# Four-block q and k loads of one head pair, moved from SyncE's queue to ScalarE's, one block a slot

## The chip, the cores and the metric

The kernel runs on one core of a Trainium2 chip. The metric is the device time of one launch in microseconds (us). The time shown for a kernel is the median of several runs; one further execution was taken with the hardware profiler, and all rows of the profile are of that one execution. PE is TensorE, DVE VectorE, ACT ScalarE, POOL GpSimd and SP SyncE. A name with a q behind it (SPq, ACTq) is the engine's instruction queue while it issues a DMA.

## The reference: hashed attention, then a gated feed-forward layer

```
# q, k, v: 4 batches, 8 heads, 768 tokens, 64 dims; proj: 64 x 6 (float32)
bits    = (q @ proj > 0), (k @ proj > 0)             # 6 bits each: a bucket of 0 to 63
mask    = q_bucket[:, None] == k_bucket[None, :]
scores  = where(mask, q @ k.T / 8, -1e9)
attn    = exp(scores - rowmax); attn /= attn.sum(-1) + 1e-9
x       = (attn @ v), heads side by side             # 3072 tokens x 512
xn      = x / sqrt(mean(x*x) + 1e-6) * rms_g
g       = xn @ w_gate                                # 512 x 1536
out     = (g * sigmoid(g) * (xn @ w_val)) @ w_out    # 3072 x 512
```

## The kernel before

**Slots.** The work is cut into 192 slots. A slot is two score matmuls (L343: 128 keys by 384 queries each) of one head and one half of a batch, called a wave w (w = 2 x batch + half). ScalarE turns them into exponentials (`probs`, L353), and TensorE multiplies these by v (L365) some slots later. Slots 0 to 47 hold batch 0, slots 48 to 71 wave 2 and slots 72 to 95 wave 3, which are the two halves of batch 1. Within a wave there are three slots a head. Slot s of the written order begins with the scores of number s+1, so `probs(54)` is issued in slot 53.

**The layer behind it.** From slot 48 on, every 24 slots carry the feed-forward layer of a finished wave: 12 gate steps (matmuls into g_ps L445, a tanh on ScalarE L447), 12 value steps (v_ps L455, two VectorE operations L457 and L458), then the output projection (y_ps L469).

**Making q and k ready.** A head pair (b, hp) of q or k is loaded as float32. For batch 0 and the first two pairs of batch 1 TensorE transposes it. From pair (1, 2) on it is loaded in four blocks of 32 partitions (`load_blocks`, L121; 768 pieces of 128 bytes each), and VectorE transposes it (`turn_dve`, L193, four operations for k and four for q); each operation reads all four blocks. GpSimd casts the result into the tile QK (L201). `hash_lone` (b = 1, hp = 2 and 3) then makes the sign bits with TensorE (d_ps L209) and VectorE (L216), and SyncE copies them into 12 rows of QK by eight small DMAs (L284). The pairs (1, 0) and (1, 1) do the same through `hash_pair`, with eight DMAs each (L267). These DMAs are called A1 to A8 for pair (1, 0) and B1 to B8 for pair (1, 1) below; A1 and A2 are needed by `scores(48)`, B1 and B2 by `scores(54)`, B3 by `scores(55)`, B4 and B5 by `scores(57)`.

**What sets the order.** The order on each engine is written out: `at(s, f, ..., rank=r)` puts a step into slot s, lower ranks first, and `probs` comes behind ranks under 3. Every engine runs its instructions in that order. The table `work` gives for each pair the slots of its k, q and v loads, of the transposes, the casts and the hash. The load tiles come from one pool of ten buffers, in turn.

**Which semaphore a DMA waits for.** As the program is built, the DMAs of SyncE and of ScalarE share eight completion semaphores, dealt out in turn over both queues together, and a DMA is not issued until the earlier DMA that holds its semaphore has landed. Before the change nearly all these DMAs are SyncE's own. A7 waits for the v load of pair (1, 1) and A8 for that of pair (1, 2). The four k blocks of pair (1, 3) follow B8 on SyncE, then come its q blocks, its v load, the k blocks of pair (2, 0) and the eight hash DMAs of pair (1, 2).

Of the kernel before, what the change touches and what calls it, by code (L numbers as in the profile page):

```python
# [43 lines left out]
def kernel(  # L44
# [12 lines left out]
    nc = tc.nc  # L57
# [38 lines left out]
    raw = {}  # L96

    def raw_tile(b, hp, which):
        shape = [128, 24, 32] if which != "v" and (b, hp) not in BY_PE else [128, 2, 6, D]
        raw[b, hp, which] = lpool.tile(shape, FP32, name=which + "L", tag="L")  # L100
        return raw[b, hp, which]
# [10 lines left out]
        else:  # L112
            eng.dma_start(out=t[:, heads[0]], in_=src[:, heads[0]])

    def load_blocks(eng, b, hp, which):
        lt = raw_tile(b, hp, which)
        for hh in range(2):
            src = {"q": q, "k": k}[which][b, 2 * hp + hh].rearrange("(t k) d -> t k d", k=24)
            for dc in range(2):
                p0 = 64 * hh + 32 * dc  # L120
                eng.dma_start(out=lt[p0 : p0 + 32], in_=src[:, :, 32 * dc : 32 * dc + 32])  # L121

# [448 lines left out]
    def at(s, f, *a, rank=3):  # L573
        plan[s].append((rank, len(plan[s]), lambda: f(*a)))
# [56 lines left out]
    def in_row(loads, s, hash_slot=None):  # L631
        return loads, range(s, s + 8), (s + 4, s + 8, s + 9), hash_slot

    work = {
        (1, 2): ((21, 23, 30), (36, 37, 40, 40, 48, 49, 50, 51), (42, 52, 46), 53),
        (1, 3): in_row((42, 44, 47), 52, 61),
        (2, 0): in_row((51, 56, 59), 61), (2, 1): in_row((64, 67, 70), 71, 80),
        (2, 2): in_row((73, 76, 79), 81), (2, 3): in_row((82, 85, 88), 91, 100),
        (3, 0): in_row((94, 98, 102), 106), (3, 1): in_row((104, 108, 112), 116, 125),
# [1 line left out]
    }  # L641
    for (b, hp), (loads, turns, cast_slots, sh) in work.items():
        for which, s in zip("kqv", loads):
            at(s, load_rows if which == "v" else load_blocks, nc.sync, b, hp, which)
        for i, s in enumerate(turns):
            at(s, turn_dve, b, hp, "kq"[i // 4], i % 4, rank=5)
        for which, s in zip("kq", cast_slots):
            at(s, cast_pool, b, hp, which)
        if sh:
            if b == 1:  # L650
                at(sh, hash_lone, b, hp)
            else:
                at(sh, hash_pairs, b, (hp - 1, hp))
        at(cast_slots[2], v_prep, b, hp)
        at(cast_slots[2], v_sum, b, hp)
        if hp % 2:
            at(66 if b == 1 else 48 * b + (17 if hp == 3 else -4), v_mean, b, hp - 1, 4)
# [100 lines left out]
```

## Time and profile before

| | us |
|---|---|
| median of 3 runs (337.58 to 343.3) | 340.42 |
| the profiled execution, its own time | 339.3 |
| its span, first to last instruction | 337.5 |
| TensorE matmul busy in it | 326.8 |
| VectorE busy | 236.4 |
| ScalarE busy | 210.0 |
| GpSimd busy | 155.3 |

The profiled execution's own time is 1.8 us longer than its span, which is what lies around the instructions. The granted TensorE clock is 0.999 over the span. Four views are used below. The busy table by stretches of time shows how full each engine is. The waits tell who waited for whom. The chain of waits goes back from the last instruction to what released each step. The timeline lists instructions in order of time: start, duration, engine, line, operation, output and input, how many were merged into the row, and in square brackets the idle time before it with its releaser. Where a row merges several, the duration is from the first start to the last end. A DMA row on SPq or ACTq is the time that the queue needed to issue it, not the transfer.

### The profile page before, as it was taken

Reading aid. Unit: us, or ns where it says so; the run is one execution under the profiler, and the core shown is the slowest. Engines: PE = TensorE matmul, PEld = TensorE weight load, DVE = VectorE, ACT = ScalarE, POOL = GpSimd, SP = SyncE. Lnnn points to the kernel's source line nnn. Section 1 sums busy time; section 2 is a strip of 40 time slices with the busy share of each in tenths; the row PEclk is TensorE's granted clock in tenths of the full one; section 3 lists DMA queues with packets and bytes.
Section 4 is the critical chain, followed back from the end, with each engine's and each line's share of the span. In section 5 each row is a group of like instructions: output and inputs, shape, how many; then the busy total and the mean of one; then the engine's idle time right before and its main releaser. Section 6 shows DMA issues by size and latency. Waiting matters only on the chain.

```text
span 337.5 us, 7796 instructions
## 1 busy us (share of the span) xinstructions
PE 326.8 (97%) x2993; PEld 201.0 (60%) x2993; DVE 236.4 (70%) x526; ACT 210.0 (62%) x328; POOL 155.3 (46%) x230
## 2 busy tenths in 40 slices
PE   8999989889999999999999999999999999999995
PEld 7566656455566565566555666566556665655653
DVE  4769798688758896668768897557546663883860
ACT  3789987656666575757666676567667675332321
POOL 4878789836465576245736475613111311110000
PEclk9999999999999999999999999999999999999999
DMA  7999999464376064508243261100010001001002
GB/s 238 330 223 260 169 169 187 75 124 100 79 186 118 15 111 119 104 20 168 69 105 84 44 116 64 35 16 0 33 62 2 3 0 64 33 0 64 32 0 93
DMA packets 80244, 31.36 MB, mean 93 GB/s; under 512 B 65240, under 2 KB 77264, under 8 KB 80208
## 3 DMA queue, kind: packets, MB, share of 16 engines
q1 hardware_dynamic: 76272, 26.09, 31.7%
q0 software_dynamic: 3712, 4.72, 8.8%
q8 instruction: 23, 0.38, 0.5%
q14 instruction: 13, 0.11, 0.1%
q10 hardware_dynamic: 224, 0.07, 0.1%
HBM read 28.32 MB, written 6.29 MB: 103 GB/s over the span
## 4 chain that ended last, share of the span: by engine, by line
PE 85%; DVE 6%; SPq 3%; DMA 2%; ACT 2%; issue 1%; DVEq 0%; ACTq 0%
PE y_ps L469 18%; PE v_ps L455 17%; PE s_ps L343 15%; PE g_ps L445 12%; PE o_ps L365 9%; PE s_ps L445 5%; PE d_ps L209 4%; SPq L267 2%; PE t_ps L169 1%; PE x_ps L430 1%; PE z_ps L336 1%; DMA kL<-in_k_dram 1%; DVE otmp L380 1%; DVE xn L423 1%; ACT psb L353 1%
## 5 line engine op out<-in xcount | busy, mean ns | idle before, releaser
L353 ACT ACTIVATE psb<-s_ps 128x768 f16<-128x768 f32 x192 | 150.8, 808 | 28.1 <-PE s_ps L343 26.9
L343 PE MATMUL s_ps<-QK 76*128 76x384 f16 x384 | 93.5, 325 | 1.3 <-ACT psb L353 0.5
L455 PE MATMUL v_ps<-xnT,wv 128*128 128x384 f16 x384 | 78.1, 326 | 0.1
L469 PE MATMUL y_ps<-wo,ht 128*128 128x512 f16 x276 | 69.2, 379 | 0.3 <-ACT ysb L476 0.3
L389 POOL TENSOR_TENSOR x<-otmp,rcp 128x384 f32<-128x384 f32 x31 | 25.7, 830 | 93.0 <-DVE rcp L385 92.7
L365 PEld LDWEIGHTS <-psb 128*128 128x128 f16 x1152 | 51.6, 97 | 25.5 <-issue 7.5
L447 ACT ACTIVATE t<-g_ps 128x384 f32<-128x384 f32 x72 | 35.3, 490 | 43.6 <-PE g_ps L445 43.4
L458 DVE SCALAR_TENSOR_TENSOR ht<-a,v_ps 128x384 f16<-128x384 f32 x96 | 53.2, 554 | 10.7 <-PE v_ps L455 1.5
L457 DVE SCALAR_TENSOR_TENSOR a<-t,g_ps 128x384 f32<-128x384 f32 x72 | 39.5, 548 | 28.5 <-ACT t L447 28.3
L445 PE MATMUL g_ps<-xnT,wg 128*128 128x384 f16 x288 | 58.6, 325 | 0.7 <-DVE a L457 0.5
L365 PE MATMUL o_ps<-vl,psb 128*128 128x65 f16 x1152 | 56.8, 194 | 0.6 <-DVE otmp L380 0.5
L455 PEld LDWEIGHTS <-wv 128*128 128x128 f16 x384 | 36.4, 97 | 23.9 <-issue 0.5
L445 PEld LDWEIGHTS <-wg 128*128 128x128 f16 x384 | 36.0, 97 | 24.4 <-issue 1.1
L343 PEld LDWEIGHTS <-QK 76*128 76x128 f16 x384 | 31.6, 98 | 16.1 <-issue 3.7
L469 PEld LDWEIGHTS <-ht 128*128 128x128 f16 x276 | 25.9, 97 | 24.0 <-issue 0.6
L476 ACT COPY ysb<-y_ps 128x512 f32<-128x512 f32 x23 | 13.5, 585 | 25.5 <-PE y_ps L469 22.8
L431 DVE TENSOR_TENSOR xnT<-x_ps,gcol 128x512 f16<-128x512 f16 x24 | 16.3, 685 | 15.1 <-PE x_ps L430 15.1
L401 POOL TENSOR_TENSOR sq<-x 128x384 f32<-128x384 f32 x31 | 25.6, 826 | 2.4
L380 DVE TENSOR_TENSOR otmp<-o_ps,cvb 128x390 f32<-128x390 f32 x32 | 17.8, 558 | 8.8 <-PE o_ps L365 8.7
L447 ACT ACTIVATE t<-s_ps 128x384 f32<-128x384 f32 x24 | 11.8, 491 | 18.4 <-PE s_ps L445 17.6
L201 POOL CAST QK<-kT 64x768 f16<-64x768 f32 x20 | 16.8, 838 | 12.4 <-DVE kT L193 6.5
L193 DVE STREAM_TRANSPOSE kT<-kL 128x192 f32<-128x192 f32 x40 | 19.8, 517 | 2.7 <-DMA kL<-in_k_dram 2.7
(80 smaller groups left out, 325.7 us busy)
## 6 DMA issues: line engine op xcount, KB each, us to landing
vL<-in_v_dram SPq DMA_DIRECT2D x16, 384.0 KB
out_dram<-ysb SPq DMA_DIRECT2D x23, 256.0 KB
kL<-in_k_dram SPq DMA_DIRECT2D x40, 96.0 KB
qL<-in_q_dram SPq DMA_DIRECT2D x40, 96.0 KB
kL<-in_k_dram SPq DMA_DIRECT2D x5, 384.0 KB
qL<-in_q_dram SPq DMA_DIRECT2D x5, 384.0 KB
wg<-in_moe_w_gate_dram POOLq DMA_DIRECT2D x2, 768.0 KB, 7.2
wv<-in_moe_w_val_dram POOLq DMA_DIRECT2D x2, 768.0 KB, 8.5
```

The costliest lines, as they stand in the source:

```text
L343: nc.tensor.matmul(ps[:, j, 0:HALF], k_cols(w // 2, h, 2 * p + j), q_cols(w, h), start=True, stop=True,)
L353: nc.scalar.activation(psb[w, h][:, p], sps.pop(g)[:, :, 0:HALF], AF.Exp, scale=ESCALE,)
L365: nc.tensor.matmul(o[:, c, hh, 0:65], psb[w, h][:, jt // 2, jt % 2, 128 * c : 128 * c + 128], vls[b % 2][:, h, v_chunk(b, h, jt), 0:65], s ...
L380: nc.vector.tensor_add(tmp[:, :, :, 0:65], o[:, :, :, 0:65], cvb[b % 2][:, 2 * hp : 2 * hp + 2, 0:65].unsqueeze(1).to_broadcast([128, 3, 2 ...
L389: eng.tensor_mul(xd.rearrange("p c (h d) -> p c h d", h=2), tmp[:, :, :, 0:64], r.to_broadcast([128, 3, 2, 64]),)
L401: nc.gpsimd.tensor_mul(sq, xd, xd)
L445: nc.tensor.matmul(g, wg[:, kt, fs], xnT[w][:, kt], start=(kt == 0), stop=(kt == 3))
L447: nc.scalar.activation(t, g, AF.Tanh, scale=0.5)
L455: nc.tensor.matmul(vv, wv[:, kt, fs], xnT[w][:, kt], start=(kt == 0), stop=(kt == 3))
L457: nc.vector.scalar_tensor_tensor(out=a, in0=t, scalar=1.0, in1=g, op0=ALU.add, op1=ALU.mult)
L458: nc.vector.scalar_tensor_tensor(out=ht[w][:, ft], in0=a, scalar=0.5, in1=vv, op0=ALU.mult, op1=ALU.mult)
L469: nc.tensor.matmul(y, ht[w][:, ft, c * 128 : (c + 1) * 128], wo[:, ft, :], start=(ft == 0), stop=(ft == NF - 1),)
```

## The change

`load_blocks` can now load some of its four blocks (`parts`), and makes the tile at the first call. Only pair (1, 3) is loaded otherwise: its k blocks are issued by ScalarE's queue in slots 46, 47, 48 and 49 and its q blocks in slots 50 to 53, one block a slot and as the last step of the slot (rank 6). Before, SyncE issued the four k blocks in slot 42 and the four q blocks in slot 44. The v load of the pair stays on SyncE in slot 47; in the pool of load tiles it now comes between k and q.

```diff
-    def load_blocks(eng, b, hp, which):
-        lt = raw_tile(b, hp, which)
-        for hh in range(2):
+    def load_blocks(eng, b, hp, which, parts=range(4)):
+        lt = raw.get((b, hp, which)) or raw_tile(b, hp, which)
+        for i in parts:
+            hh, dc = divmod(i, 2)
             src = {"q": q, "k": k}[which][b, 2 * hp + hh].rearrange("(t k) d -> t k d", k=24)
-            for dc in range(2):
-                p0 = 64 * hh + 32 * dc
-                eng.dma_start(out=lt[p0 : p0 + 32], in_=src[:, :, 32 * dc : 32 * dc + 32])
+            eng.dma_start(out=lt[32 * i : 32 * i + 32], in_=src[:, :, 32 * dc : 32 * dc + 32])
...
-        (1, 3): in_row((42, 44, 47), 52, 61),
+        (1, 3): in_row((46, 50, 47), 52, 61),
...
-            at(s, load_rows if which == "v" else load_blocks, nc.sync, b, hp, which)
+            if which == "v":
+                at(s, load_rows, nc.sync, b, hp, which)
+            elif (b, hp) == (1, 3):
+                for i in range(4):
+                    at(s + i, load_blocks, nc.scalar, b, hp, which, [i], rank=6)
+            else:
+                at(s, load_blocks, nc.sync, b, hp, which)
```

The order of the compute instructions on TensorE, VectorE, ScalarE and GpSimd is the same in both built programs; the eight loads go from SyncE's list into ScalarE's. On ScalarE the order there becomes: `probs(47)`, k0, `probs(48)`, k1, tanh 0, `probs(49)`, k2, tanh 1, `probs(50)`, k3, `probs(51)`, tanh 2, q0, `probs(52)`, q1, tanh 3, `probs(53)`, q2, tanh 4, `probs(54)`, q3, `probs(55)`, tanh 5, `probs(56)`, where k0 to q3 are the blocks.

The eight semaphores are dealt out anew, now over both queues. As built, these DMAs wait for these to have landed:

| DMA (queue) | waits for the landing of |
|---|---|
| k0 (ACT) | a k block of pair (1, 2), issued 20 slots earlier |
| A7 (SP) | v load of pair (1, 2) |
| A8 (SP) | k0 |
| k1 (ACT) | A2 |
| k2 (ACT) | k1 |
| k3 (ACT) | B3 |
| q0 (ACT) | B4 |
| q1 (ACT) | B7 |
| q2 (ACT) | k2 |
| q3 (ACT) | q0 |
| fourth k block of pair (2, 0) (SP) | v load of pair (1, 3) |
| first hash DMA of pair (1, 2) (SP) | k3 |

## The prediction

> **What bounds the kernel now.** I read the busy totals first, then the waits, then the chain, then the timelines of single engines.
>
> ```profile
> PE 326.8 (97%) x2993; PEld 201.0 (60%) x2993; DVE 236.4 (70%) x526; ACT 210.0 (62%) x328; POOL 155.3 (46%) x230
> ```
>
> TensorE is busy for 326.8 of 337.5 us. A change that only moves loads can win no more than idle time of TensorE. The busy table by stretches shows where there is some near the change.
>
> ```profile
> 50.00:57.20 7.20, 6.52 (x80) 4.39 (x80) 5.87 (x10) 5.34 (x8) 6.70 (x10) 1.00 1.20 224
> 57.20:61.50 4.30, 4.30 (x43) 2.79 (x42) 3.85 (x10) 3.58 (x7) 4.14 (x6) 1.00 0.12 25
> 61.50:66.60 5.10, 5.10 (x49) 2.63 (x47) 2.84 (x7) 3.32 (x6) 4.81 (x8) 1.00 0.61 97
> 66.60:69.10 2.50, 0.34 (x2) 0.12 (x2) 1.77 (x4) 0.25 (x1) 0.34 (x1) 1.00 0.96 144
> 69.10:76.00 6.90, 6.90 (x65) 4.47 (x65) 6.02 (x14) 4.30 (x8) 2.80 (x4) 1.00 0.58 116
> ```
>
> The columns are the stretch, its length, busy PE, PEld, DVE, ACT and POOL, granted clock, DMA share, GB/s. TensorE is full from 57.2 to 66.6 and again from 69.1; in the 2.50 us between it works 0.34. So 2.16 us are the prize. The waits from 57 to 76 us name the cause:
>
> ```profile
> DVE kT L193 <- DMA kL<-in_k_dram: 2.7, 1, 2.7
> PE m_ps L324 <- DVE bits L216: 1.6, 1, 1.6
> PE g_ps L445 <- DVE a L457: 0.5, 1, 0.5
> ```
>
> VectorE waits 2.7 us for k of pair (1, 3), and TensorE behind it 1.6 + 0.5. The chain tells why k is late:
>
> ```profile
> 60.56 0.72 SPq L267
> ...
> 61.39 0.65 SPq L121
> ...
> 63.86 3.29 DMA kL<-in_k_dram
> ...
> 67.28 0.52 DVE kT L193
> 67.79 0.45 DVE bits L216
> ...
> 69.10 0.82 PE g_ps L445 x4
> ...
> 72.83 1.79 DMA QK<-bits
> ```
>
> SyncE issues hash DMAs up to B8 at 60.56 and only then the k blocks. A block lands 3.29 us after its issue begins, a hash DMA 1.79.
>
> **Part 1: what SyncE loses, and its new wait.** Its timeline and one of its waits:
>
> ```profile
> 54.42 6.86 SPq L267 DMA_DIRECT2D QK<-bits  x9
> ...
> 61.39 3.06 SPq L121 DMA_DIRECT2D kL<-in_k_dram  x4
> 64.56 2.64 SPq L121 DMA_DIRECT2D qL<-in_q_dram  x4
> ...
> 71.15 6.18 SPq L284 DMA_DIRECT2D QK<-bits  x8
> ```
> ```profile
> SPq L267 <- DMA vL<-in_v_dram: 2.3, 1, 2.3
> ```
>
> Eight issues leave SyncE, 61.39 to 67.20, so 5.8 us of its queue. But A8, the first of the nine at 54.42, will wait for k0. The nine take 6.86/9 = 0.76 us each, so B3 is issued 3 x 0.76 = 2.28 after A8 and lands 1.79 later: 4.1 us after k0 has landed.
>
> When k0 lands follows from ScalarE's timeline and the weight load beside it:
>
> ```profile
> 50.94 3.66 ACT L353 ACTIVATE psb<-s_ps 128x768 f16<-128x768 f32 x5 [0.38 <-PE s_ps L343]
> 55.13 0.81 ACT L353 ACTIVATE psb<-s_ps 128x768 f16<-128x768 f32 x1 [0.53 <-PE s_ps L343]
> ```
> ```profile
> 47.75 0.82 POOL L526 DMA_DIRECT2D wo<-in_moe_w_out_dram  x1
> ```
> ```profile
> wo<-in_moe_w_out_dram POOLq DMA_DIRECT2D x2, 768.0 KB, 10.3
> ```
>
> The five are `probs(43)` to `probs(47)`; k0 stands behind them, so its issue begins at 50.94 + 3.66 = 54.60. The nearest price of a landing is 3.29, which gives 57.9. But the DMA engines are full to 57.2 (share 1.20) with a weight load that lands at 47.75 + 10.3 = 58.05, while the 3.29 was taken at a share of 0.61 to 0.96. If none of k0's data moved before that load is done, the 1.50 by which a block (3.29) is longer than a hash DMA (1.79) comes on top: 59.5. I take 58.3, just behind the weight load, with 57.9 and 59.5 as bounds. Then B3 lands at 58.3 + 4.1 = 62.4. Between A8's old issue at 54.42 and its new one at 58.3 SyncE stands still for 3.9 us and gives back most of its 5.8. Two score rows of TensorE, `scores(53)` and `scores(54)`, tell whether that hurts at once:
>
> ```profile
> 61.47 0.49 PE L343 MATMUL s_ps<-QK 76*128 76x384 f16 x2
> ...
> 63.37 0.49 PE L343 MATMUL s_ps<-QK 76*128 76x384 f16 x2
> ```
>
> B1 and B2 land by 58.35 + 2 x 0.76 + 1.79 = 61.7, before `scores(54)` at 63.4, so TensorE does not feel it directly.
>
> **Part 2: what ScalarE gains to do.** An issue on ACTq occurs twice in the trace, for other shapes:
>
> ```profile
> 0.72 0.55 ACTq L483 DMA_DIRECT2D pn<-in_proj_dram  x1
> ```
> ```profile
> 334.47 0.35 ACTq L726 DMA_DIRECT2D out_dram<-ysb  x1
> ```
>
> SyncE paid 0.65 for this shape (the L121 row). Bounds are 0.35 and 0.65 in calm queues; I take 0.65, the same shape. Eight are 5.2 us. The cover is ScalarE's idle time, in brackets below, some tenths at a time and 3.10 in the old stall:
>
> ```profile
> 57.27 0.81 ACT L353 ACTIVATE psb<-s_ps 128x768 f16<-128x768 f32 x1
> 58.51 0.49 ACT L447 ACTIVATE t<-g_ps 128x384 f32<-128x384 f32 x1 [0.44 <-PE g_ps L445]
> 58.90 1.51 ACT L353 ACTIVATE psb<-s_ps 128x768 f16<-128x768 f32 x2
> 60.69 0.49 ACT L447 ACTIVATE t<-g_ps 128x384 f32<-128x384 f32 x1 [0.28 <-PE g_ps L445]
> ...
> 66.04 0.81 ACT L353 ACTIVATE psb<-s_ps 128x768 f16<-128x768 f32 x1 [0.30 <-PE s_ps L343]
> 69.95 0.49 ACT L447 ACTIVATE t<-g_ps 128x384 f32<-128x384 f32 x1 [3.10 <-PE g_ps L445]
> 70.33 0.81 ACT L353 ACTIVATE psb<-s_ps 128x768 f16<-128x768 f32 x1
> ```
>
> A tanh holds the next instruction back 0.39 (58.51 to 58.90), a probs 0.75 (1.51/2). Now step by step:
> - k0 from 54.60 to 55.25 moves `probs(48)` by 0.1, k1 runs 56.06 to 56.71 in a gap. No cost.
> - k2 needs k1: 56.06 + 3.29 = 59.35, issued to 60.00. Tanh 1 moves from 58.51 to 60.00 and `probs(50)` ends at 60.00 + 0.39 + 0.75 = 61.14. ScalarE is 1.5 late, but the next wait covers this one.
> - k3 needs B3: issued 62.4 to 63.05. `probs(51)` ends at 63.8 instead of 58.90 + 1.51 = 60.41. Queued behind k3 are tanh 2 and everything later on ScalarE; TensorE has two score banks, so `scores(53)` needs the bank that `probs(51)` frees. It moves from 61.5 to 63.8: TensorE stands 2.3 us, in the place of the old 2.16.
> - From 63.05 to the start of `probs(56)` ScalarE runs without a gap: five probs (51 to 55), four tanh (2 to 5), four issues (q0 to q3): 5 x 0.75 + 4 x 0.39 + 4 x 0.65 = 7.9, so 70.95. It was 70.33: 0.6 late. q0 and q1 add no wait: B4 and B7 land at 63.2 and 65.4, ScalarE arrives at 64.2 and 65.6; q2 and q3 wait for blocks issued more than 3.29 us before.
>
> TensorE agrees: its 5.1 us of work from 61.5 to 66.6, begun at 63.8, ends at 68.9, and the gate step of 69.10 follows some tenths later, since tanh 4 and VectorE's chain to it are as late as ScalarE. After that `scores` and gates have slack on ScalarE (busy 4.30 of 6.90 from 69.1), and TensorE is full, so the 0.6 stays to the end and does not grow.
>
> **Part 3: what comes with it.** k is complete at 62.4 + 3.29 = 65.7, before 67.15, and VectorE's first transpose no longer waits for it; q3, issued at about 69.6, lands by 73, before the q transposes. The hash DMAs of (1, 2) begin near 70, a little before 71.15. The v load of (1, 3) and k of (2, 0) each move by under 2 us and have slots to spare: 0. The swapped pool buffers were released over 15 slots earlier: 0.
>
> The Trainium skill (DMA: Bandwidth & Descriptors, Issuing engines are not separate DMA queues) says that issuing from several engines saves only the sequencer's time to initiate. By it alone, SyncE would be 5.8 us freer, k early, and the whole 2.16 saved. The same page (Anatomy of one DMA) puts a semaphore wait on the issuing sequencer before dispatch, which SyncE's 2.3 us wait above agrees with; by that rule the 2.16 is paid again on ScalarE.
>
> **The sum.** Old stall -2.16, new stall and issues +2.8, net +0.6: 339.3 + 0.6 = 339.9 by the profiled execution. That execution is 1.1 below the median of 340.42, so for a median I say 341.0.
>
> **Rivals.**
> - Faster: ScalarE's issues cost 0.35 and overlap, k0 lands at 57.9 or the waits are met earlier still. With 57.9 and 0.35, k3 ends at 62.35, q1 waits for B7 until 65.0, and `probs(56)` starts at 69.5: -0.8. If no wait on ScalarE binds at all, all 2.16 comes back: 338.3 on the median. (This last is what the page's rule on issuing engines would give.) For it: two ACTq rows at 0.35 and 0.55. Against: A8 cannot go before k0 lands, as built.
> - Slower: ScalarE's issue is long when both queues issue at once. The four k blocks of pair (1, 2) show such a price on SyncE:
>
> ```profile
> 34.62 6.73 SPq L121 DMA_DIRECT2D kL<-in_k_dram  x4
> ```
>
>   That is 1.7 each. On ScalarE five issues from k3 on stand in the gapless stretch: +5 x 1.03 = 5.2 on top of 0.6, so 346.2. It passes 2% (6.8 us) from 1.9 us an issue. Against: the DMA share is 0.12 from 57.2 to 61.5, far from full. A smaller form, k0 at 59.5 and 0.9 an issue, gives 0.6 + 1.2 + 5 x 0.25 = 3.05: 343.5.
> - The change does nothing visible: the stall moves from VectorE's wait to ScalarE's, and the two cancel within some tenths. That is my forecast's lower half.
>
> **Chances.** Forecast (0 to +1.5): 0.52. Faster rival (below 0): 0.2. Slower rival (+1.5 and more): 0.23, of it 0.07 with issues over 1.9 us; something unseen, likely slower, 0.05. The range, 338.0 to 344.5, holds the first two and the smaller form of the third; the runs of before alone span 337.6 to 343.3. The forecast's own range is 340.4 to 342. A 2% difference is about what a measurement of this kernel can tell from no change. Faster by over 2% would need 6.8 us, three times the prize, so only the spread of runs could show it: 0.04, out of the faster rival. Slower by 2% is 0.07 + 0.05 = 0.12. Within: 0.84.
>
> **What would show it.** Right: on ScalarE two new idle stretches ahead of L120, the larger one before k3, ended by a hash DMA; SyncE idle near 55 to 58 before A8, ended by k0; TensorE's gap at 66.6 gone, and one near 61.5 to 63.8 ahead of s_ps in its place. Wrong: k0 landing far from 58.3, ACTq rows far from 0.65, or a TensorE gap elsewhere after 70 us.

## The result, and the profile after

Median of 13 runs each, on the same chip: 338.2 us before (337.21 to 343.3), 342.23 us after (339.86 to 343.9). The ratio is 1.0121, 95% interval 1.0091 to 1.015: about 4 us slower, within 2%. Ratios here leave out disturbed executions, so they need not be the quotient of the medians. The profiled execution of the changed kernel took 343.33 us, its span is 341.6, its granted clock 0.988 (before: 339.3, 337.5, 0.999). Line numbers are now lower by one: probs is L352, scores L342, the gate step L444, `load_blocks` L120.

The busy table by stretches, changed kernel (stretch, length, PE, PEld, DVE, ACT, POOL, granted clock, DMA share, GB/s):

```profile
61.50:65.10 3.60, 1.11 (x6) 0.58 (x6) 1.88 (x5) 0.84 (x2) 3.37 (x6) 0.82 0.20 35
65.10:70.70 5.60, 5.58 (x25) 2.72 (x24) 3.08 (x6) 2.24 (x4) 1.85 (x3) 0.50 0.83 165
```

TensorE works 1.11 us in the first 3.60, and then 5.58 of 5.60 at half its clock. Before, it was full from 61.5 to 66.6 at 1.00 and all but stood from 66.6 to 69.1. TensorE's largest wait from 50 to 90 us, and SyncE's:

```profile
PE s_ps L342 <- ACT psb L352: 3.6, 3, 2.5
```
```profile
SPq L266 <- DMA kL<-in_k_dram: 5.3, 1, 5.3
```

VectorE's wait for k (2.7 us before) and TensorE's at m_ps are gone. In their place stand SyncE for k0 (5.3), ScalarE for two hash DMAs (2.83 and 2.01, in the timeline below) and TensorE for `probs`. The chain of waits shows them as one line of dependence:

```profile
53.95 5.37 DMA kL<-in_k_dram
...
59.34 0.71 SPq L266
...
61.68 1.88 DMA QK<-bits
...
63.59 0.57 ACTq L120
...
64.25 0.82 ACT psb L352
...
65.11 0.80 PE s_ps L342 x2
```

k0 lands at 59.32, A8 is issued, B3 lands at 63.56, k3 is issued, `probs(51)` runs, `scores(53)` follows. ScalarE's timeline shows how issues and activations lie:

```profile
50.97 3.66 ACT L352 ACTIVATE psb<-s_ps 128x768 f16<-128x768 f32 x5 [0.38 <-PE s_ps L342]
53.95 0.64 ACTq L120 DMA_DIRECT2D kL<-in_k_dram  x1
...
59.61 0.57 ACTq L120 DMA_DIRECT2D kL<-in_k_dram  x1
60.23 0.49 ACT L446 ACTIVATE t<-g_ps 128x384 f32<-128x384 f32 x1 [2.15 <-PE o_ps L364]
...
64.25 0.81 ACT L352 ACTIVATE psb<-s_ps 128x768 f16<-128x768 f32 x1 [2.83 <-DMA QK<-bits]
64.36 0.58 ACTq L120 DMA_DIRECT2D qL<-in_q_dram  x1
...
67.49 0.57 ACTq L120 DMA_DIRECT2D qL<-in_q_dram  x1
68.16 0.49 ACT L446 ACTIVATE t<-g_ps 128x384 f32<-128x384 f32 x1 [2.01 <-DMA QK<-bits]
```

The five `probs` end at 54.63, yet k0 is issued from 53.95: an issue starts inside the activation ahead of it. So does q0 at 64.36, within the `probs` of 64.25. ScalarE stops three times: 2.15 us at k2 (its bracket names o_ps, but the tanh follows the issue of k2 at 59.61, and by the table above k2 waits for k1, issued at 54.94), 2.83 at k3 and 2.01 at q1. An issue that had to wait holds back the activation behind it by its whole length: from 59.61 to 60.23, from 63.59 to 64.25 and from 67.49 to 68.16. On TensorE:

```profile
61.47 0.49 PE L342 MATMUL s_ps<-QK 76*128 76x384 f16 x2 [0.81 <-ACT psb L352]
...
65.11 0.80 PE L342 MATMUL s_ps<-QK 76*128 76x384 f16 x2 [2.51 <-ACT psb L352]
65.71 1.49 PE L444 MATMUL g_ps<-xnT,wg 128*128 128x384 f16 x4
...
73.23 0.81 PE L444 MATMUL g_ps<-xnT,wg 128*128 128x384 f16 x4
```

The stop at k2 costs TensorE the gap of 0.81 us, the stop at k3 the gap of 2.51. A gate step takes 1.49 instead of 0.81 while the clock is low. The row at 73.23 is the gate step behind m_ps, which began at 69.10 before: 4.13 later, the whole difference of the spans (4.1). It is the mark by which the runs below are compared, and is called the marked gate step.

### The profile page after: what moved, and what is told of

It is laid out like the page before. It is cut to its first block, busy times and chain, and to the rows that moved or that the text cites. A ratio compares the mean times of both kernels' runs of the same rounds, so it can differ in the third digit from the quotient of the medians.

```text
span 341.6 us, 7794 instructions
## 1 busy us (share of the span) xinstructions
PE 329.5 (96%) x2993; PEld 201.8 (59%) x2993; DVE 236.9 (69%) x526; ACT 210.1 (62%) x328; POOL 155.4 (45%) x230
## 4 chain that ended last, share of the span: by engine, by line
PE 87%; DVE 4%; DMA 3%; ACT 1%; POOL 1%; issue 1%; SPq 1%; ACTq 0%; DVEq 0%; POOLq 0%
PE v_ps L454 18%; PE y_ps L468 18%; PE s_ps L342 16%; PE g_ps L444 14%; PE o_ps L364 10%; PE s_ps L444 5%; PE d_ps L208 4%; DMA kL<-in_k_dram 2%; PE t_ps L168 1%; PE x_ps L429 1%; PE z_ps L335 1%; DVE otmp L379 1%; ACT psb L352 1%; SPq L266 1%; DMA out_dram<-ysb 1%
## 5 line engine op out<-in xcount | busy, mean ns | idle before, releaser
L352 ACT ACTIVATE psb<-s_ps 128x768 f16<-128x768 f32 x192 | 150.9, 808 | 30.7 <-PE s_ps L342 26.6
L342 PE MATMUL s_ps<-QK 76*128 76x384 f16 x384 | 94.1, 327 | 4.5 <-ACT psb L352 4.1
L444 PE MATMUL g_ps<-xnT,wg 128*128 128x384 f16 x288 | 59.8, 330 | 0.6 <-DVE xnT L430 0.4
L444 PEld LDWEIGHTS <-wg 128*128 128x128 f16 x384 | 36.4, 98 | 25.2 <-issue 2.3
L342 PEld LDWEIGHTS <-QK 76*128 76x128 f16 x384 | 31.6, 98 | 19.9 <-issue 6.6
L200 POOL CAST QK<-qT 64x768 f16<-64x768 f32 x20 | 16.7, 835 | 10.8 <-DVE qT L192 10.2
```

The costliest lines, as they stand in the source:

```text
L200: nc.gpsimd.tensor_copy(QK[b, hp][0:64, hh, o : o + S], T0[b, hp, which][64 * hh : 64 * hh + 64, :])
L342: nc.tensor.matmul(ps[:, j, 0:HALF], k_cols(w // 2, h, 2 * p + j), q_cols(w, h), start=True, stop=True,)
L352: nc.scalar.activation(psb[w, h][:, p], sps.pop(g)[:, :, 0:HALF], AF.Exp, scale=ESCALE,)
L444: nc.tensor.matmul(g, wg[:, kt, fs], xnT[w][:, kt], start=(kt == 0), stop=(kt == 3))
```

## The experiments

**1. How large was the prize? The kernel before, profiled again.** Nothing is edited.

> The kernel before once more, unchanged, for a second profile. The first one took 339.3 us, 1.8 more than the median of 29 later runs of the same kernel (337.47). Theory: in a typical run the old stall (TensorE waiting at m_ps for the sign bits, 1.65 + 0.51 us) is there as in the first profile, because SyncE's order and A8's wait for the v load are in the program; then m_ps waits 1.3 to 2.0 us and the 1.8 us lie elsewhere. Rival: the stall itself is what varies, since it hangs on when the v load and the k blocks land beside the weight load; then a run near 337.5 shows m_ps waiting under 0.7 us, and the prize that the change could win was never 2.16 in a typical run.

It took 337.26 us, span 335.5. Its TensorE rows at the place of the old stall, SyncE's row of the k blocks, and SyncE's wait:

```profile
65.95 0.81 PE L455 MATMUL v_ps<-xnT,wv 128*128 128x384 f16 x4
66.60 0.28 PE L324 MATMUL m_ps<-vsum,ones 128*128 128x260 f16 x1
67.03 0.81 PE L445 MATMUL g_ps<-xnT,wg 128*128 128x384 f16 x4
```
```profile
59.54 3.05 SPq L121 DMA_DIRECT2D kL<-in_k_dram  x4
```
```profile
SPq L267 <- DMA vL<-in_v_dram: 1.8, 1, 1.8
```

No wait stands in brackets at m_ps. A8's wait for the v load is there (1.8 instead of 2.3), but SyncE began its 16 hash DMAs at 45.29 instead of 46.65 and came to the k blocks at 59.54 instead of 61.39, and VectorE did not wait for them. The rival holds: the stall varies from run to run. The medians of the kernel before were 337.4 to 338.4 in the four sessions, so the execution with the stall (339.3) was 1 to 2 us above a usual one. By this profile a usual one has no 2.16 us to win, and the marked gate step of 67.03 is the base to compare with.

**2. How much is waiting, how much is the clock?** The changed kernel, with 40 idle matmuls on TensorE that fill the gap ahead of `scores(53)`; no DMA is touched. They write columns that nothing reads.

```
+    spare = []
...
+        if g == 52:
+            spare.append(ps)                     # in scores()
...
+    at(51, lambda: idle(spare[0][:, 0, HALF:512], 40), rank=2.9)
```

> The changed kernel with 40 extra 128x128 matmuls on TensorE (their result is never read), put ahead of scores(53), where TensorE stood idle for 2.5 us before its clock fell to 0.50. Waits, loads and queues are those of the changed kernel. Theory (the gap costs twice: once as idle time and once as a halved clock for the 5.6 us behind it): the extra matmuls fill the gap, the clock stays at 1.00 and about 2.5 us of the change's 4 us loss come back, so about 1.005 of the kernel before, or 339.7. Rival (the clock fell for another reason, and the loss is all waiting): no gain, 342, ratio 1.012.

340.9 us against 337.47, ratio 1.0084 (1.0052 to 1.0116); profile span 338.9, clock 1.00.

```profile
61.37 2.40 PE L336 MATMUL s_ps<-ones 128*128 128x128 f16 x40
...
67.60 0.51 PE L208 MATMUL d_ps<-kT,pk 128*32 128x384 f32 x1 [0.94 <-DVE a L459]
...
70.08 0.81 PE L447 MATMUL g_ps<-xnT,wg 128*128 128x384 f16 x4
```
```profile
61.40:63.70 2.30, 2.30 (x42) 2.30 (x41) 0.59 (x2) 0.93 (x2) 2.14 (x5) 1.00 0.08 17
```

TensorE is busy through the place of the gap, `scores(53)` follows the filler, and the clock does not fall. The mean granted clock is 1.00 in ten of the 12 runs; the other two, 345.63 and 345.37 us at 0.99, left no trace. About 1.3 us of the loss came back (1.0121 to 1.0084), which lies between the two forecasts, 2.5 and nothing.

The marked gate step stands at 70.08, 3.05 behind the usual run of before. Of these, 2.05 us are that `scores(53)` starts at 63.63 instead of 61.58; most of the rest is the new gap of 0.94 ahead of d_ps, behind the tanh that q1 held up (ScalarE stood 1.81 us for it). The gate step is 3.15 ahead of the changed kernel's profile, but not all of that is the clock: A8 resumed at 57.85, so k0 landed 1.5 us earlier here and `scores(53)` came 1.48 earlier. Only the other 1.67 arose behind it. So waiting is worth about 3 us, and the fall of the clock, where it occurs, about 2 (1.9 by the means that follow).

It does not occur in each run. Of the 13 of the changed kernel five have a mean granted clock of 1.00 (339.86 to 342.74, mean 341.1) and eight 0.988 to 0.995 (342.17 to 343.9, mean 342.95). The eight are of two kinds: three with 0.993 to 0.995 (mean 342.2) and five with 0.988 to 0.990 (mean 343.4).

**3. The changed kernel, profiled again.**

> The changed kernel once more, for a second profile. Theory: the wait for k3 and TensorE's gap of 2 to 2.6 us ahead of scores(53) are there in every run, as they are in the program; what differs between runs is whether the granted clock falls to 0.50 behind it. So either the clock stays 1.00, gate step 5 starts near 70.3 us and the run takes 340 to 342, or it falls again, 73 us and 342 to 344. Rival: the gap itself differs, by over 1 us, and the clock follows it.

342.65 us, span 340.8. First a row of the chain, then TensorE's gap, then the busy table:

```profile
53.87 5.80 DMA kL<-in_k_dram
```
```profile
65.47 0.48 PE L342 MATMUL s_ps<-QK 76*128 76x384 f16 x2 [2.33 <-ACT psb L352]
```
```profile
66.40:68.70 2.30, 2.30 (x18) 1.24 (x16) 0.99 (x2) 0.59 (x3) 1.10 (x2) 0.56 0.58 141
68.70:70.20 1.50, 1.50 (x9) 0.54 (x11) 1.36 (x3) 0.74 (x3) 0.54 (x1) 0.53 1.14 236
```

The gap is there again, 2.33 (2.51 in the first profile), and k0 takes 5.80. The clock fell about a microsecond after TensorE had resumed; 0.56 and 0.53 in these stretches are 3.4 us at 0.50. The marked gate step is at 72.53. The theory holds: the wait is in the program, the moment of the fall is not.

**4. A gap without any DMA moved.** The kernel before, with 16 exponentials of weight values on ScalarE ahead of `probs(51)`.

```
+        if g == 51:
+            spare.append(ps)                     # in scores()
...
+    def hold(n):
+        for _ in range(n):
+            nc.scalar.activation(
+                spare[0][:, :, HALF:512], wg[:, 0:2, 0 : 512 - HALF], AF.Exp, scale=ESCALE)
...
+    at(50, hold, 16, rank=0)
```

> The kernel before with no DMA moved, and 16 exponentials of 128 x 256 weight values put on ScalarE ahead of probs(51), into columns of a score bank that nothing reads. From the rows of 384 and 768 columns (0.39 and 0.75 us) they take about 0.27 each, 4.3 in all, about what the wait for k3 delayed probs(51) by in the changed kernel. Theory (a late probs(51) costs what it holds up on TensorE, whatever makes it late, and the idle time then drops the clock): a TensorE gap of 2.2 to 2.8 us ahead of scores(53); granted clock 0.50 for some 5 us behind it in part of the runs; 340.5 to 343, ratio 1.008 to 1.016. Rival (the clock and the loss come with the DMAs on ScalarE's queue): clock 1.00 in all runs, under 340, ratio 1.002 to 1.006.

344.87 us against 337.39, ratio 1.0202 (1.015 to 1.0255); mean clock 0.988 to 0.995 in all six runs.

```profile
59.75 6.69 ACT L648 ACTIVATE s_ps<-wg 128x256 f32<-128x256 f16 x16
```
```profile
67.33 0.80 PE L345 MATMUL s_ps<-QK 76*128 76x384 f16 x2 [5.54 <-ACT psb L357]
```
```profile
67.30:71.20 3.90, 3.87 (x20) 2.09 (x20) 2.10 (x4) 2.25 (x4) 1.64 (x2) 0.50 0.65 94
```

The size missed, since each activation took 0.42 instead of 0.27, so the gap is 5.54 instead of 2.5. No DMA is on ScalarE's queue near this place, and the clock falls to 0.50 all the same, within the gap, and is low for 3.9 us behind it. So idle time alone can drop it, without those DMAs. That a gap of the changed kernel's size does so without them is not shown, since this one is twice as long.

The Trainium skill (TensorE: Matmul & The Clock Gate, Part 1: The HAM clock gate) says that TensorE goes to half rate after an idle window of about 3.4 us, that the window is "free-running", and that it takes such a window of work to come back. The traces agree on the way back, very closely: cut into steps of 0.1 us, the clock is low from 63.8 to 70.6 in the first profile of the change, from 66.7 to 70.1 in experiment 3 and from 64.4 to 71.3 here, which is 6.8, 3.4 and 6.8 us, one or two times 3.4. The profiles with a low clock of experiments 5, 8 and 9 have 3.4 us each. The two kinds of runs in experiment 2 fit this: 3.4 us at half clock make a mean of 0.995 over 340 us, 6.8 us one of 0.990. The first kind costs the changed kernel about 1.1 us, the second about 2.3. On the way down the traces need less than the Trainium skill says. A gap of 5.54 drops the clock in all six runs, but the gaps of the changed kernel (0.81 and 2.51, 1.12 and 2.33), all shorter than 3.4, drop it in eight of 13, and a single gap of 2.75 did so in experiment 5.

**5. What does issuing by ScalarE cost?** The changed kernel with the k blocks two slots later (48 to 51), where the DMAs that they inherit their semaphores from have landed; the q blocks go back to SyncE, the v load follows in slot 56.

```
-        (1, 3): in_row((46, 50, 47), 52, 61),
+        (1, 3): in_row((48, 52, 56), 52, 61),
...
-            elif (b, hp) == (1, 3):
+            elif (b, hp) == (1, 3) and which == "k":
```

> k of pair (1, 3) on ScalarE's queue one a slot as in the change, but in slots 48 to 51; q back on SyncE in slot 52, v in slot 56. As built, the four k blocks now wait for A8, two of the B DMAs and k0, which by the trace of before have landed when ScalarE comes to them; no A or B DMA waits for a k block. Theory (the loss comes from ScalarE and SyncE waiting for each other's DMAs, not from issuing on ScalarE): no idle stretch of over 0.5 us on ScalarE ahead of the blocks, old stall gone or under 0.5 us, 336.5, ratio 0.994. Rival (an issue on ScalarE costs its 0.57 us each and holds up the exponentials): half the change's loss, ratio 1.005.

338.3 us against 337.47, ratio 1.0005 (0.9973 to 1.0037). The forecast ratios, 0.994 and 1.005, both missed. The profiled run is its slowest (342.55, mean clock 0.995) and has a wait of TensorE for GpSimd, with the clock low from 58.2 to 61.6 behind it:

```profile
58.05 0.68 PE L342 MATMUL s_ps<-QK 76*128 76x384 f16 x2 [2.75 <-POOL x L388]
```

A second profile does not have this wait:

> The same kernel as k48act (k blocks on ScalarE in slots 48 to 51, where the DMAs they wait for have landed; q blocks on SyncE), for a second profile, as the first one had a wait of TensorE for GpSimd near 58 us. Theory: no wait of ScalarE for a DMA over 0.5 us, ACTq rows of 0.57 to 0.65 us that begin inside the exponential ahead of them, and VectorE's wait for k under 1.5 us: about 337 to 338.5. Rival (issuing by ScalarE costs its 0.6 us each in sequence): four gaps of about 0.6 us ahead of the activation behind each issue, and TensorE waiting for a score bank.

337.62 us, span 335.8.

```profile
57.79 0.49 ACT L446 ACTIVATE t<-g_ps 128x384 f32<-128x384 f32 x1 [0.44 <-PE g_ps L444]
57.79 0.58 ACTq L120 DMA_DIRECT2D kL<-in_k_dram  x1
58.17 1.51 ACT L352 ACTIVATE psb<-s_ps 128x768 f16<-128x768 f32 x2
59.96 0.49 ACT L446 ACTIVATE t<-g_ps 128x384 f32<-128x384 f32 x1 [0.28 <-PE g_ps L444]
59.97 0.57 ACTq L120 DMA_DIRECT2D kL<-in_k_dram  x1
60.58 0.81 ACT L352 ACTIVATE psb<-s_ps 128x768 f16<-128x768 f32 x1
```
```profile
66.60 0.29 PE L323 MATMUL m_ps<-vsum,ones 128*128 128x260 f16 x1 [0.68 <-DVE bits L215]
```

The issue begins with the tanh ahead of it. At 57.79 the next `probs` follows 0.38 later, as without an issue; at 59.96 it follows 0.62 later, so 0.24 is paid. ScalarE waits for no DMA. An issue whose semaphore is free costs it 0 to 0.24 us here. VectorE waits 1.8 for k, more than the 1.5 that was expected, as the blocks are issued later, and TensorE's stall at m_ps is back in part: 0.68 us there and 0.51 at the marked gate step, which starts at 67.41, 0.38 behind that of experiment 1. So nothing is won, but nothing like the change's 4 us is lost.

**6. Same slots, same queue, other partners.** The changed kernel, with the v load of pair (1, 2) moved behind. As built, A8 then waits for the v load of (1, 1), k0 for B2 and k3 for B6.

```
-        (1, 2): ((21, 23, 30), (36, 37, 40, 40, 48, 49, 50, 51), (42, 52, 46), 53),
+        (1, 2): ((21, 23, 43), (36, 37, 40, 40, 48, 49, 50, 51), (42, 52, 53), 53),
```

> The changed kernel, same blocks, queue and slots, with the v load of pair (1, 2) moved from slot 30 to 43 on SyncE (its preparation from 46 to 53). That alone deals the semaphores differently: A8 waits for the v load of pair (1, 1), not for k0; k0 waits for B2, k1 for B4, k2 for B5, k3 for B6, which by SyncE's pace (16 hash DMAs without a stop, 45.2 to 57.6 us in the kernel with this edit alone) have landed by 54 to 58 us, before ScalarE comes to them. Theory (the loss is ScalarE standing for k3 behind B3, A8 and k0, plus the clock that falls after TensorE's gap): no wait of ScalarE over 0.6 us, no gap at scores(53), granted clock 1.00, 336.5 to 338 us, ratio 0.995 to 1.001. Rival (what costs is that ScalarE issues at all, or that q and k come late): ratio 1.007 or more, as the change itself.

338.72 us against 337.39, ratio 1.0022 (0.9986 to 1.0058); profile span 336.4, clock 0.999.

```profile
45.27 6.54 DMA QK<-bits
```
```profile
57.50 0.81 ACT L352 ACTIVATE psb<-s_ps 128x768 f16<-128x768 f32 x1 [3.13 <-DMA QK<-bits]
...
62.54 0.81 ACT L352 ACTIVATE psb<-s_ps 128x768 f16<-128x768 f32 x1 [0.34 <-issue]
```
```profile
68.09 0.81 PE L444 MATMUL g_ps<-xnT,wg 128*128 128x384 f16 x4 [0.16 <-DVE a L456]
```

The loss against the kernel before falls from 1.2% to 0.2%, and the interval holds 1. With the queue and the slots the same, only the dealing and the place of one v load differ, so the rival (1.007 or more) is out. But that v load alone gains 0.4% (experiment 10, 0.9964). Against that kernel the change still costs about 0.6% (1.0022/0.9964 = 1.0058; the two ratios come from different sessions). So the new dealing removes about half of the loss by this count, and what is left is again a wait, at least in part: `probs(48)` stood 3.13 us behind k0, and TensorE felt 1.11 of it; the marked gate step is 1.06 behind that of experiment 1. As built, k0 waits for B2, and B2 for A2. A2, at 45.27, took 6.54 us; B2 was issued at 51.83 and k0 only at 56.76, so B2 took up to 4.9, where a hash DMA of the kernel before took 1.79. Both lay beside the weight load (DMA share 1.02 to 1.25 from 44 to 56 us). That wait was not expected, and the ratio is just above the theory's 0.995 to 1.001. At 62.54 an issue that waited for nothing costs ScalarE about 0.44 (0.83 behind the tanh instead of 0.39).

**7. One slot later.** The changed kernel with (47, 51, 47) for (46, 50, 47): A8 waits for the v load of (1, 2) again, k3 for the v load of (1, 3).

> The changed kernel with each of the eight blocks one slot later on ScalarE (47 to 54). The semaphores are dealt out anew: A8 waits for the v load of (1, 2) as in the kernel before, k0 for B2, k1 for B4, k2 for B7, k3 for the v load of pair (1, 3), q1 and q3 for k blocks of pair (2, 0). Theory (whoever's semaphore a block inherits sets the cost): A8 and k0 do not wait, k2 under 1 us, but the v load is issued behind B8 near 60 us and lands 3 or more later, so k3 waits 2 to 3.5 us and TensorE stands 1.5 to 3 us, now one slot later, ahead of scores(54); ratio 1.006 to 1.014. Rival (A8 behind k0 was the whole cause): no gap over 1 us, ratio under 1.003.

340.98 us against 337.39, ratio 1.0094 (1.0058 to 1.0131). Its profile is of the shortest of its ten runs (339.43):

```profile
67.47 0.29 PE L323 MATMUL m_ps<-vsum,ones 128*128 128x260 f16 x1 [0.95 <-DVE bits L215]
68.27 0.81 PE L444 MATMUL g_ps<-xnT,wg 128*128 128x384 f16 x4 [0.51 <-DVE a L456]
```

That A8 behind k0 was the whole cause is out: A8 no longer waits for a block, and the kernel is as slow as expected. But the gap forecast ahead of `scores(54)` is not in this trace. ScalarE lost 1.44 us ahead of the activation behind k3, VectorE waited 1.56 us ahead of its first k transpose, and the wait at m_ps (0.95 and 0.51) is back. What the runs near 341 us stood for, no trace shows.

**8. The slots without ScalarE's queue.** The changed kernel with `nc.sync` for `nc.scalar`.

> The changed kernel with all eight blocks issued by SyncE in the same slots 46 to 53: the slots without the other queue. SyncE's order becomes k0, v load, k1, k2, k3, q0, four k blocks of (2, 0), q1, q2, then the hash DMAs of pair (1, 2), q3, where before all eight blocks stood ahead of it. ScalarE has no DMA and so no wait for one. Theory (the loss of the change lies in ScalarE standing in line for k3 behind B3, A8 and k0): no gap at scores(53), the clock stays at 1.00 there, k one issue later than before, so the old stall at m_ps grows from 2.16 to about 2.8: ratio 1.000 to 1.003, 337.5 to 338.5. Rival (the loss comes from the later slots themselves, blocks and hash DMAs landing later): ratio 1.006 to 1.012, with VectorE waiting for q blocks or TensorE for the hash rows of pair (1, 2).

344.35 us against 338.35, ratio 1.0199 (1.017 to 1.0227). Rows of SyncE, VectorE and TensorE:

```profile
67.42 7.06 SPq L283 DMA_DIRECT2D QK<-bits  x8
74.52 3.43 SPq L120 DMA_DIRECT2D qL<-in_q_dram  x5
```
```profile
77.28 0.52 DVE L192 STREAM_TRANSPOSE qT<-qL 128x192 f32<-128x192 f32 x1 [4.77 <-DMA qL<-in_q_dram]
```
```profile
79.00 1.44 PE L454 MATMUL v_ps<-xnT,wv 128*128 128x384 f16 x4 [4.83 <-DVE a L456]
```

The theory missed. The rival's mechanism held, at more than its number (1.006 to 1.012). The last q block stands behind the eight hash DMAs of pair (1, 2) on SyncE, VectorE waits 4.77 us for it and TensorE 4.83, and the clock is low behind that gap too (a value step takes 1.44). On SyncE, the late slots alone are worse than the change; ScalarE's queue spares q3 that line, as it was issued at 70.88 there.

**9. Two other variants.** The change on GpSimd's queue (`nc.gpsimd` for `nc.scalar`), and the kernel before with the k blocks in slot 40 instead of 42, ahead of B's hash DMAs.

> The changed kernel with the same eight blocks at the same slots issued by GpSimd's queue instead of ScalarE's. GpSimd's DMAs have completion semaphores of their own, so no A or B DMA waits for a block and no block waits for an A or B DMA. Theory (the shared semaphores make the loss): no stall on ScalarE, clock at 1.00; k comes when GpSimd gets to it, behind its casts, so the old stall may stay in part: 336.5 to 339, ratio 0.995 to 1.003. Rival (taking the blocks off SyncE or the new slots make the loss): as the change, ratio 1.01.

343.58 us, ratio 1.0162 (1.0104 to 1.022). A wait that neither theory had named decides its profile: `scores` stood 4.27 us at 59.46 for a hash DMA, with the clock low behind it. Both forecasts missed, and the run says nothing of ScalarE.

> The kernel before with one number changed: SyncE issues the four k blocks of pair (1, 3) in slot 40 instead of 42, which puts them between A8 and B1 in its queue. ScalarE issues nothing. Theory (the prize is the 2.16 us stall for k, and it needs no second queue): k lands before VectorE asks for it, B1 and B2 still land before scores(54), 336.0, ratio 0.994. Rival (the B DMAs, 2.7 us later, become the wait that TensorE meets): no gain or a loss, 338 to 340.

341.12 us, ratio 1.008 (1.0044 to 1.0116). In its profile TensorE waits for a hash DMA itself:

```profile
PE s_ps L343 <- DMA QK<-bits: 1.4, 1, 1.4
```

That profile is of one of its three shortest runs (338.99). Putting the blocks earlier on the same queue makes the hash DMAs late; the rival held, at more than its 338 to 340.

**10. The kernel before with the v load moved alone** (the edit of experiment 6, nothing on ScalarE).

> The kernel before, with one edit: the v load of pair (1, 2) comes behind the k blocks of pair (1, 3) on SyncE (slot 43 instead of 30), and its preparation moves from slot 46 to 53. So A8 no longer waits for that load, and nothing is issued by ScalarE. Theory (the k blocks are late since A8 to B8 stand ahead of them and A8 waits 2.3 us): k of pair (1, 3) lands about 2 us sooner, VectorE's wait of 2.7 falls under 1, TensorE's 2.16 us stall goes, and no new wait comes: 335.5 to 336.5 against a median of 337.5 for the kernel before, ratio 0.994 to 0.998. Rival (the stall is shorter in a typical run, or the DMA engines rather than SyncE's queue hold the blocks back): ratio 0.999 to 1.002. Slower, 1.004 and more, if v of pair (1, 2) is now late for the value matmuls of its head in wave 2 (a TensorE wait at o_ps near 64 us).

337.05 us against 338.35, ratio 0.9964 (0.9938 to 0.999). All 12 runs lie between 336.43 and 338.01. SyncE and TensorE:

```profile
45.21 12.43 SPq L267 DMA_DIRECT2D QK<-bits  x16
57.74 3.46 SPq L121 DMA_DIRECT2D kL<-in_k_dram  x4
```
```profile
67.00 0.28 PE L324 MATMUL m_ps<-vsum,ones 128*128 128x260 f16 x1
```

The 16 hash DMAs take 12.43 us instead of 14.63, the k blocks start at 57.74, and m_ps does not wait. This is the one version that beats both kernels, the one before by 0.1 to 0.6%. That it is so little fits a stall that only some runs of the kernel before have.

## Why the prediction was right or wrong

The range (338.0 to 344.5) and the class (within 2%) held. The time came out 1.2 us above the 341.0, and beyond the forecast's own range of 340.4 to 342. That it came so near is luck: the change itself was forecast at +0.6 us and measured at +4.0. Two large errors cancelled. By the medians: the base was taken as 340.42 and is 338.2 (-2.2); the prize was taken as 2.16 and is about nothing in a usual run (+2.2); the new waits were +2.8 and are about 3 (+0.2); the clock was not in the sum and adds 8 of 13 x 1.9 = 1.2. Together +1.4, against 1.2 measured.

- **The prize, step one: wrong.** The 2.16 us were read rightly from one trace, but from one trace only. The runs shown with it went from 337.58 to 343.3, a spread of over twice the prize, and the profiled 339.3 stood 1.7 above the lowest; experiment 1 has no stall.
- **The base: wrong.** Adding 1.1 us to get from the profiled execution to a median of three put the base above that of every later session.
- **Part 1, the mechanism: right.** A8 waits for k0, k3 for B3, and the stall of TensorE moves to `scores(53)`: 2.51 and 2.33 against the 2.3 forecast. From k0's landing to B3's it was 4.24 (forecast 4.1). The stop at k2 came as forecast too (issued at 59.61, forecast 59.35) and, as forecast, the next one covers its time; it splits TensorE's idle time into 0.81 and 2.51.
- **Part 1, k0's landing: mis-sized.** Issued at 53.95, not 54.60, it landed at 59.32 and in the second profile at 59.67, not 58.3: 5.37 and 5.80 us instead of 3.7, just under and beyond the upper bound (59.5). SyncE stood 5.3 us instead of 3.9. In experiment 2 A8 resumed at 57.85, at the lower bound, so this too varies. What made k0 so slow no run separates.
- **Part 2, the price of an issue: wrong.** Taken as 0.65 in sequence, four times behind k3. The rows are 0.57 to 0.64, as bounded, but those that wait for nothing lie inside the activation ahead of them, and little is paid (0 to 0.24 in experiment 5). In full, 0.62 to 0.67, it is paid only where the issue had to wait: k2, k3 and q1. The slower rival, long issues, did not occur in the changed kernel. The step of a `probs` was also read a little high: 1.51/2 counts half of the last one's tail, and the five in 3.66 us follow each other by 0.71.
- **Part 2, q1: missed.** "q0 and q1 add no wait" failed, by 2.1 us: B7 was to land at 65.4, and q1 was issued at 67.49. About 1.0 of that is k0's later landing, which moves A8 and B7 alike; the rest is B7's own landing, about 2.75 after its issue at 64.71 instead of 1.79 (2.55 in experiment 2). ScalarE stood 2.01 us for it. So what followed `scores(53)` was not the 2.6 us of issues but this wait, which cost TensorE 0.94 in experiment 2; the total of 2.8 came out nearly right for the wrong reason.
- **Part 3: right.** k no longer makes VectorE wait, and q3 is in time. The hash DMAs of (1, 2) began at 72.43 instead of near 70; no wait of TensorE for them shows in the trace.
- **Not foreseen: the clock.** The stall was expected to cost its length. The stall of 2.16 us in the first trace left the clock at 1.00, and the text asked no more. The new one is 2.51 long and has 0.81 us of idle time just ahead of it with little work between, and in eight of 13 runs the clock fell. Whether it is the length or the pair that matters no run separates; the single gap of 2.75 in experiment 5 shows that a pair is not needed.

The Trainium skill's rule on issuing engines (DMA: Bandwidth & Descriptors, Issuing engines are not separate DMA queues: only the sequencer's time is saved) was weighed for the faster rival. The Trainium skill's rule that a semaphore wait happens on the issuing sequencer (the same page, Anatomy of one DMA) decided. The traces agree with the second: SyncE's 5.3 us and ScalarE's 2.83 are waits ahead of an issue.

## What to carry to other kernels

A DMA that moves to another queue takes its semaphore's history along: list for each moved DMA and for those dealt after it whose landing it waits for, and when that landing comes, before counting what the issue costs. Take a stall for a prize only when a second profile shows it, above all where the runs spread by more than the stall. And price a gap on TensorE with the clock that may fall behind it: here 3 us of waiting came, in eight of 13 runs, with one or two stretches of 3.4 us at half clock, which cost about 1.1 or 2.3 us more.

## What the runs showed of the hardware that was not expected

- ScalarE's DMA issue runs beside the activation ahead of it: 0.57 to 0.64 us long in the changed kernel, beginning up to 0.7 us before that activation ends (53.95 against 54.63). With a free semaphore 0 to 0.24 us is paid in experiment 5 and up to 0.44 in experiment 6; an issue that had to wait is paid in full (0.62 to 0.67).
- The granted clock fell with gaps of 2.33 to 2.75 us, inside the gap in one profile (63.8, in the gap that ends at 65.11) and a microsecond after work had resumed in another (66.7, resumed at 65.47), and stayed at 0.50 for 3.4 or 6.8 us in all six profiles in which it fell in the middle of the run.
- Small DMAs beside a large weight load: a hash DMA that takes 1.8 to 1.9 us later on took 6.54 us at 45.27 (experiment 6), and a k block about 4.0 to 5.80 instead of 3.29 (k0, in three profiles). That the load is the cause is argued from the DMA share; no run moves it.
